# Gated mix of linear attention and a gated MLP: two buffers for x chunks, low parts in place, h blocks and last weights at other places of the order

## The chip, the cores and the metric

The kernel runs on one core of a Trainium2 chip, in one launch. The metric is device time in microseconds (us). The engines are named as in the profile: PE (TensorE matmul), DVE (VectorE), ACT (ScalarE), POOL (GpSimd) and SP (SyncE, which only issues DMAs here).

## The reference

The input `x` is 2048 tokens by 576. A linear attention with 32 heads of 18 and a gated MLP with 4608 hidden columns both read it, and a sigmoid gate mixes them.

```python
g = sigmoid((x * gate_w).sum(-1, keepdims=True))
q, k, v = heads(x @ wqkv)                      # 32 heads of 18
phi = lambda t: where(t > 0, t + 1, exp(t)) + 1e-6
kv = einsum("bhsd,bhse->bhde", phi(k), v);  z = phi(k).sum(s)
o = einsum("bhqd,bhde->bhqe", phi(q), kv) / (einsum("bhqd,bhd->bhq", phi(q), z) + 1e-6)
a = o.reshape(B, S, D) @ wo
b = (gelu(x @ w_gate) * (x @ w_up)) @ w_down
return g * a + (1 - g) * b
```

## The kernel before

All matrices are float32. The operands of PE are `float32r`, each split into a high part and a low part (value minus high part), and a product is summed from three of the four combinations. The three large products of the MLP use a seven-product scheme for 2x2 blocks (Strassen's, `PRODUCTS`, in the order of `SEQUENCE`): the sums of x blocks that it needs (S1 to S4), of weight blocks (T1 to T4) and of h blocks (S1 to S4 again) are formed on POOL and DVE.

The order of work on each engine is the order in which the program names it: nothing is rearranged, and each engine takes its instructions in that order. An instruction waits until its inputs are there and its output buffer is free, and all behind it on its engine wait too. DMAs issued by SP are in this order as well; a few are issued by ACT.

**The mixing stage** (lines 368 to 919). Queries of the four token blocks (512 tokens each, `query(b, g)` for five groups of heads), their denominators (`den`), the reciprocals of these, the scaled queries and the mixed output (`mixed(b, t)`, 128 tokens) are interleaved by hand, block 2 first, then 3, 0 and 1. `halves_of` splits a query for `den`. `reciprocals(b)` works on halves of a block: it stores a small tile to memory (L638) and reloads it spread over the rows of each head (L642, tile `rb`). `scaled` multiplies (L654) and splits (L65, L66) for `mixed` (PE, L673), whose result ACT scales by the gate and stores (`ga_d`, L678, L680).

Beside these, two things are prepared for the MLP:

* *Ahead chunks* 0 to 5: the sums of x blocks of the second half of the tokens, in pieces of 256 columns. `ahead_load(k)` loads a raw chunk (tile `xu`, two buffers, L388). `ahead_make(k)` forms the four sums in it on POOL (L378 to L381), copies high parts to `xuh` (L397, one buffer) and writes low parts to `xul` (L399, one buffer; for the chunks 4 and 5 into rows of `xuh`, L401). `ahead_store(k)` stores low (L408) and high parts (L409) to `xop_d`. `next_ahead(k)` is: store k-1, load k+1, make k.
* *Token chunks* 0 to 2 of the first half (tile `xc`, 128 x 4 x 512, one buffer, L608). `token_sums(kt, 0)` forms the sums on DVE; `token_sums(kt, 1)` copies high parts on ACT (L612) and low parts on POOL (L615) into `xo`, the operand of the first products.

`W[0]` and `W[1]`, the split and summed weights of gate and up, are loaded by ACT's queue for the first columns (L769, L912) into the place of the query weights.

**Gate and up** (lines 976 to 1012). `CHAINS` lists chains of seven products (L810), of GATE or UP, for token halves p = 0 and 1 and 18 pairs of column groups n; the last two chains are (1, 0, GATE) and (1, 0, UP), for which the weights of n = 0 come back from memory: `w_load(0)` behind the first product of chain LAST - 3, `w_load(1)` behind the last of LAST - 2, both on SP. Results of UP chains go to memory as h blocks (`h_d`, L841). `H_AT` names the places in the last two chains where the first four h blocks of the down product are split (`h_make`: ACT L978, DVE L979), each followed by a load of a later one (L973).

**Down** (lines 1013 to 1076). 84 units: six groups s of hidden columns, token halves p, seven products k; a unit is 36 matmuls (L1049) in two halves. Three units ahead, `h_make(u + 3)` splits an h block between the halves of a unit. The down weights of a group come in one load into `draw` (`d_fetch`, L955), are split and summed by `d_make(s, k)` (ACT copy L960, POOL low parts L962; for k = 0 also six POOL operations L965 that form sums in `draw` which later makes read; for k = 2 two). Products are accumulated on DVE (L1057), and ACT copies the result of the first product of a seven to a second bank (L1053).

Of the kernel before, what the change touches and what calls it, by code (L numbers as in the profile page):

```python
# [38 lines left out]
def tile_gated_mix(ctx, tc, xt, xs, xn, wk, wv, wq, wo, wgu, wdn, cst, out):  # L39
    nc = tc.nc  # L40
# [12 lines left out]
    def f32(ap):  # L53
        return ap.bitcast(F32)
# [318 lines left out]
    xup = mixing.pool("xup")  # L373
# [11 lines left out]
    def ahead_load(k):  # L385
        kt, c = k // 2, slice(k % 2 * 256, k % 2 * 256 + 256)
        raw = xup.tile([128, 4, 256], F32, name="xu", bufs=2)
        nc.sync.dma_start(raw, xs[1, kt, :, :, c])  # L388
        ahead[k] = [raw]

    def ahead_make(k):
        kt, (raw,) = k // 2, ahead[k]
        sum_blocks(raw, nc.gpsimd)
        hi = xup.tile([128, 4, 256], F32R, name="xuh")
        lo = xup.tile([128, 4, 256], F32R, name="xul") if kt < 2 else None
        for i in range(4):
            nc.gpsimd.tensor_copy(hi[:, i], raw[:, i])  # L397
            if kt < 2:
                nc.gpsimd.tensor_tensor(lo[:, i], raw[:, i], f32(hi[:, i]), OP.subtract)  # L399
            else:  # L400
                nc.gpsimd.tensor_tensor(hi[32:64, i], raw[32:64, i], f32(hi[32:64, i]), OP.subtract)  # L401
        ahead[k] = [hi, lo]

    def ahead_store(k):
        kt, c = k // 2, slice(k % 2 * 256, k % 2 * 256 + 256)
        hi, lo = ahead.pop(k)
        if kt < 2:
            nc.sync.dma_start(xop_d[:, S2:S1 + 1, 3 + kt, c], f32(lo))  # L408
        nc.sync.dma_start(xop_d[:, S2:S1 + 1, kt, c], f32(hi))  # L409

    def next_ahead(k):
        ahead_store(k - 1)
        if k < 5:
            ahead_load(k + 1)
        if k < 6:
            ahead_make(k)

# [159 lines left out]
    for k in range(2):  # L577
        ahead_load(k)
# [7 lines left out]
    for g in range(NG):  # L586
        if g + 1 < NG:
            query(3, g + 1)
        head_out(g)
        if g + 2 < NG:  # L590
            wo_load(g + 2)
        elif g + 2 == NG:
            for b, i, a in ((2, 0, A11), (2, 1, A12), (3, 1, A22)):
                nc.sync.dma_start(xop_d[:, a], f32(x_slot(b, i)))
        den(2, g)
        if g + 2 < NG:
            halves_of(2, g + 2)
    turn.close()
    weights.close()
    ahead_make(0)  # L600
# [26 lines left out]
    xcp = chunks.pool("xcp")  # L627
# [54 lines left out]
    chunk = [Chunk(xcp, 0, 0)]  # L682

    def token_load(kt):
        chunk[0] = Chunk(xcp, 0, kt)

    def token_sums(kt, part):
        if part == 0:
            chunk[0].sums()
        else:  # L690
            chunk[0].summed(nc.gpsimd)
# [3 lines left out]
    halves_of(3, 1)  # L695
    query(0, 0)
    query(0, 1)
    next_ahead(1)
# [4 lines left out]
    query(0, 2)  # L703
    den(3, 2)
# [4 lines left out]
    next_ahead(2)  # L709
    den(3, 4)  # L710
    scaled(2, 1)
    mixed(2, 0)
    reciprocals(3)
# [4 lines left out]
    next_ahead(3)  # L718
# [4 lines left out]
    query(1, 0)  # L723
    mixed(2, 2)
    ahead_store(3)
    ahead_load(5)
    token_load(1)
    ahead_make(4)
# [6 lines left out]
    mixed(2, 3)  # L735
    scaled(3, 1)
# [9 lines left out]
    ahead_store(4)  # L746
# [3 lines left out]
    token_load(2)  # L750
    ahead_make(5)
# [3 lines left out]
    query(1, 4)  # L755
    proj.close()
# [20 lines left out]
    ahead_store(5)  # L777
# [49 lines left out]
    def w_load(m):  # L827
        nc.sync.dma_start(f32(W[m]), wp_d[m])
# [154 lines left out]
    H_AT = [(LAST - 1, 1), (LAST - 1, 5), (LAST, 2), (LAST, 5)]  # L983
# [4 lines left out]
    for c, chain in enumerate(CHAINS):  # L988
        for i, step in enumerate(first_steps if c == 0 else gu_steps(*chain)):
# [10 lines left out]
            if i == 0 and c == LAST - 3:  # L1000
                w_load(0)
            if i == 6 and c == LAST - 2:
                w_load(1)
# [57 lines left out]
    for u, (s, p, k) in enumerate(UNITS):  # L1061
# [10 lines left out]
        if s < DG - 1:  # L1072
            if p == 0 and k == 3:
                d_fetch(s + 1)
            if p == 0 and k == 5:
                d_make(s + 1, 0)
# [65 lines left out]
```

## Time and profile before

| | |
|---|---|
| median of 3 runs | 1551.15 us (1545.82 to 1554.31) |
| the profiled execution | 1548.94 us, span 1547.2 us |
| busy time: PE, DVE, ACT, POOL | 1504.2 (97%), 1006.3 (65%), 539.0 (35%), 736.7 (48%) us |
| DMA | 248.19 MB, mean 160 GB/s |
| granted clock of PE, mean | 0.99 |

The page gives for each group of instructions its line, engine, output and inputs; the list of waits gives who stood for whom, with the total, the count and the longest in us. In a timeline a line is: start, duration (us), engine, line, operation, tiles and shapes, how many instructions are merged, and in brackets the idle time of that engine before it and what ended it. A row of windows is: the stretch, its length, busy time of PE, weight loads, DVE, ACT and POOL with their counts, the granted clock, the share of time in which the DMA engines were busy, and GB/s.

### The profile page before, as it was taken

The numbers are of one execution on the slowest core, as the hardware profiler recorded it, in microseconds if no ns is written. First come the engines' busy times: TensorE is split into PE (matmuls) and PEld (weight loads), VectorE is DVE, ScalarE is ACT, GpSimd is POOL, SyncE is SP. The second block draws the span as 40 slices with busy tenths as digits, with TensorE's granted clock in tenths as the row PEclk, the third lists the DMA queues.
The fourth block names the chain that finished last, engine by engine and source line by source line (L and its number), as shares of the span: only waits on it lengthen the run. The fifth ranks groups of instructions, "written<-read, shape, count | busy, mean of one in ns | idle before, by whom it ended". The sixth has DMA issues, their size and how long they took to land.

```text
span 1547.2 us, 21598 instructions
## 1 busy us (share of the span) xinstructions
PE 1504.2 (97%) x8354; PEld 1327.9 (86%) x8354; DVE 1006.3 (65%) x1314; ACT 539.0 (35%) x703; POOL 736.7 (48%) x560
## 2 busy tenths in 40 slices
PE   8999996799999999999999999999998999999999
PEld 8998875788788888888888888888788999999999
DVE  7886755456655666655566665556766776777775
ACT  6554543332233222223322223322244343534431
POOL 3653467164554454455456446444346282552700
PEclk9999997899999999999999999999999999999999
DMA  7554355574222333222233322233777656565664
GB/s 238 164 160 157 124 175 189 184 277 191 104 106 101 129 137 136 103 103 102 103 136 136 119 102 106 108 111 116 277 275 266 207 172 209 164 209 167 212 204 139
DMA packets 99310, 248.19 MB, mean 160 GB/s; under 512 B 8960, under 2 KB 38296, under 8 KB 96264
## 3 DMA queue, kind: packets, MB, share of 16 engines
q1 hardware_dynamic: 96328, 237.26, 44.6%
q10 hardware_dynamic: 2880, 9.57, 1.7%
q8 instruction: 65, 1.06, 0.3%
q14 instruction: 37, 0.30, 0.1%
HBM read 157.24 MB, written 89.55 MB: 160 GB/s over the span
## 4 chain that ended last, share of the span: by engine, by line
PE 83%; DMA 5%; DVE 3%; POOL 3%; issue 3%; ACT 1%; SPq 0%; DVEq 0%; POOLq 0%; ACTq 0%
PE bank L810 50%; PE bank L1049 24%; PE pair L244 2%; PE kpair L244 2%; DMA xc<-xs 1%; PE bank L432 1%; PE kpair L199 1%; PE pair L199 1%; POOL xul L399 1%; DMA stage<-wdn 1%; DMA rb<-rden_d 1%; POOL xuh L397 1%; PE pair L673 1%; DMA rden_d<-rb 1%; DMA wu<-wp_d 1%
## 5 line engine op out<-in xcount | busy, mean ns | idle before, releaser
L810 PE MATMUL bank<-xo,wg 128*128 128x512 f32 x1764 | 413.9, 395 | 3.2 <-DVE f L845 1.5
L810 PE MATMUL bank<-xo,wu 128*128 128x512 f32 x1764 | 412.8, 394 | 3.0 <-DMA wu<-wp_d 3.0
L810 PEld LDWEIGHTS bank<-xo,wg 128*128 128x128 f32 x1764 | 332.1, 189 | 81.1 <-DVE f L845 1.9
L810 PEld LDWEIGHTS bank<-xo,wu 128*128 128x128 f32 x1764 | 332.5, 189 | 80.3 <-DMA wu<-wp_d 3.5
L1057 DVE SCALAR_TENSOR_TENSOR acc<-bank,gate,acc 128x288 f32<-128x288 f32 x288 | 140.4, 511 | 76.0 <-PE bank L1049 67.6
L818 POOL TENSOR_TENSOR stage<-stage 128x384 f32<-128x384 f32 x136 | 159.6, 1193 | 46.7 <-DMA stage<-wgu 44.1
L824 POOL TENSOR_TENSOR wg<-stage,wg 128x768 fp32r<-128x768 f32 (+1 forms) x34 | 72.2, 2123 | 192.4 <-ACT wg L823 191.1
L854 ACT ACTIVATE p<-bank 128x512 f32<-128x512 f32 x72 | 43.2, 600 | 344.6 <-PE bank L810 344.6
L824 POOL TENSOR_TENSOR wu<-stage,wu 128x768 fp32r<-128x768 f32 (+1 forms) x34 | 79.7, 2344 | 146.2 <-ACT wu L823 144.9
L1049 PE MATMUL bank<-xo 128*128 128x288 f32 x1044 | 142.6, 296 | 4.8 <-DVE acc L1057 4.1
L1049 PEld LDWEIGHTS bank<-xo 128*128 128x128 f32 x1044 | 140.3, 189 | 5.3 <-DVE acc L1057 4.4
L962 POOL TENSOR_TENSOR wd<-stage,wd 128x432 fp32r<-128x432 f32 x40 | 58.4, 1483 | 130.8 <-ACT wd L960 130.7
L859 DVE TENSOR_TENSOR u<-bank,p 128x512 f32<-128x512 f32 x72 | 49.5, 687 | 99.5 <-PE bank L810 94.0
L1049 PE MATMUL bank<-wd,xo 128*128 128x288 f32 x792 | 106.8, 296 | 0.0
L1049 PEld LDWEIGHTS bank<-wd,xo 128*128 128x128 f32 x792 | 105.6, 188 | 0.0
L962 POOL TENSOR_TENSOR xo<-stage,xo 128x432 fp32r<-128x432 f32 x44 | 56.7, 1315 | 82.1 <-ACT xo L960 82.1
L845 DVE TENSOR_TENSOR e<-bank,u 128x512 f32<-128x512 f32 x54 | 37.3, 691 | 80.0 <-PE bank L810 79.7
L845 DVE TENSOR_TENSOR f<-bank,u 128x512 f32<-128x512 f32 x54 | 37.2, 691 | 76.1 <-PE bank L810 76.0
L835 ACT ACTIVATE f<-f 128x512 f32<-128x512 f32 x54 | 34.1, 632 | 140.9 <-DVE f L845 140.9
L673 PE MATMUL pair<-kw,p 126*128 126x288 f32 (+1 forms) x480 | 72.0, 310 | 8.2 <-ACT p L65 8.1
L673 PEld LDWEIGHTS pair<-kw,p 126*128 126x128 f32 (+1 forms) x480 | 70.3, 202 | 10.5 <-ACT p L65 8.5
L873 DVE TENSOR_TENSOR u<-bank,u 128x512 f32<-128x512 f32 x72 | 49.8, 691 | 38.8 <-PE bank L810 37.0
(189 smaller groups left out, 2315.9 us busy)
## 6 DMA issues: line engine op xcount, KB each, us to landing
h_d<-sx SPq DMA_DIRECT2D x108, 256.0 KB
stage<-wgu SPq DMA_DIRECT2D x34, 768.0 KB
xo<-h_d SPq DMA_DIRECT2D x29, 768.0 KB
e<-h_d SPq DMA_DIRECT2D x28, 768.0 KB
hraw<-h_d SPq DMA_DIRECT2D x27, 768.0 KB
h_d<-e SPq DMA_DIRECT2D x72, 256.0 KB
h_d<-f SPq DMA_DIRECT2D x72, 256.0 KB
stage<-wdn SPq DMA_DIRECT2D x6, 1728.0 KB
```

What stands on the lines that cost most here:

```text
L244: nc.tensor.matmul(y[:, n, :KH], a, p[:, n * KH:(n + 1) * KH], start=(k == 0), stop=(k == len(ops) - 1))
L673: nc.tensor.matmul(y[:, i, :288], p[:R, a, g], KW[g][:R, wl, i * 288:(i + 1) * 288], start=(n == 0), stop=(n == 14))
L810: nc.tensor.matmul(ps, w_, x_, start=start and i == 0, stop=i == 6, skip_group_check=not start)
L818: nc.gpsimd.tensor_tensor(o, a, b, OP.subtract)
L824: nc.gpsimd.tensor_tensor(w[:, i, 3:5], src[:, :, 0:2], f32(w[:, i, 0:2]), OP.subtract)
L845: nc.vector.tensor_tensor(es[i], a, b, OP.add)
L854: nc.scalar.activation(p1, ps["a"], AF.Copy)
L859: nc.vector.tensor_tensor(u2, b, p1, OP.add)
L873: nc.vector.tensor_tensor(u3, c, u2, OP.add)
L962: nc.gpsimd.tensor_tensor(w[:, 1, c], src[:, c], f32(w[:, 0, c]), OP.subtract)
L1049: nc.tensor.matmul(y, h[:, hl, g, t * 128:(t + 1) * 128], w[:, wl, g * 288:(g + 1) * 288], start=k in (1, 5) and n == 0, stop=n == len(ops ...
L1057: nc.vector.scalar_tensor_tensor(o, y, gate[:, 1, st:st + 1], o, op0=OP.mult, op1=OP.add)
```

## The change

* Mixing: `xcp` has two buffers, and `token_load(1)` and `token_load(2)` are issued earlier. `xul` is gone: low parts of the chunks 0 to 3 are written over the raw chunk and stored from there. The ahead pool moves to the place of the `raws` pool, next to the query weights, so its first two loads are issued once `raws` is closed. The stores of A12 and A22 to `xop_d` move from the loop before to behind `halves_of(3, 1)` and `query(0, 1)`. The places of makes, loads and stores in the order are others, and all go by `next_ahead`.
* End of gate and up: `H_AT` has later places, and `w_load(1)` is issued by ACT behind the first product of chain LAST - 1.
* Down: `d_fetch(s + 1)` is one unit later, and `d_make(s + 1, 0)` two units later, directly ahead of `d_make(s + 1, 1)`.
* `dynamic_dma_scratch_size` is 512 instead of 1024.

```diff
@@ -370,7 +370,6 @@
     mixing.banks(3)
     denp = mixing.psum("denp", 1)
     rp = mixing.pool("rp", bufs=2)
-    xup = mixing.pool("xup")
     made = Scope()
     r_of = {}
     def sum_blocks(raw, eng):
@@ -384,37 +383,33 @@
 
     def ahead_load(k):
         kt, c = k // 2, slice(k % 2 * 256, k % 2 * 256 + 256)
-        raw = xup.tile([128, 4, 256], F32, name="xu", bufs=2)
+        raw = xup.tile([128, 4, 256], F32, name="xu")
         nc.sync.dma_start(raw, xs[1, kt, :, :, c])
         ahead[k] = [raw]
 
     def ahead_make(k):
         kt, (raw,) = k // 2, ahead[k]
         sum_blocks(raw, nc.gpsimd)
-        hi = xup.tile([128, 4, 256], F32R, name="xuh")
-        lo = xup.tile([128, 4, 256], F32R, name="xul") if kt < 2 else None
+        hi = xup.tile([128, 4, 256], F32R, name="xuh", bufs=1)
         for i in range(4):
             nc.gpsimd.tensor_copy(hi[:, i], raw[:, i])
-            if kt < 2:
-                nc.gpsimd.tensor_tensor(lo[:, i], raw[:, i], f32(hi[:, i]), OP.subtract)
-            else:
-                nc.gpsimd.tensor_tensor(hi[32:64, i], raw[32:64, i], f32(hi[32:64, i]), OP.subtract)
-        ahead[k] = [hi, lo]
+            o = raw[:, i].bitcast(F32R) if kt < 2 else hi[32:64, i]
+            p = slice(0, 128) if kt < 2 else slice(32, 64)
+            nc.gpsimd.tensor_tensor(o, raw[p, i], f32(hi[p, i]), OP.subtract)
+        ahead[k] = [hi, raw]
 
     def ahead_store(k):
         kt, c = k // 2, slice(k % 2 * 256, k % 2 * 256 + 256)
         hi, lo = ahead.pop(k)
         if kt < 2:
-            nc.sync.dma_start(xop_d[:, S2:S1 + 1, 3 + kt, c], f32(lo))
+            nc.sync.dma_start(xop_d[:, S2:S1 + 1, 3 + kt, c], lo)
         nc.sync.dma_start(xop_d[:, S2:S1 + 1, kt, c], f32(hi))
 
     def next_ahead(k):
         ahead_store(k - 1)
         if k < 5:
             ahead_load(k + 1)
-        if k < 6:
-            ahead_make(k)
-
+        ahead_make(k)
 
     def wv_make(kt):
         raw = wv_raw.pop(kt)
@@ -574,8 +569,6 @@
 
     wo_load(0)
     wo_load(1)
-    for k in range(2):
-        ahead_load(k)
     query(2, 3)
     states_out()
     key_sums()
@@ -590,14 +583,16 @@
         if g + 2 < NG:
             wo_load(g + 2)
         elif g + 2 == NG:
-            for b, i, a in ((2, 0, A11), (2, 1, A12), (3, 1, A22)):
-                nc.sync.dma_start(xop_d[:, a], f32(x_slot(b, i)))
+            nc.sync.dma_start(xop_d[:, A11], f32(x_slot(2, 0)))
         den(2, g)
         if g + 2 < NG:
             halves_of(2, g + 2)
     turn.close()
     weights.close()
-    ahead_make(0)
+    aheads = Scope()
+    xup = aheads.pool("xup", bufs=2, side="right")
+    for k in range(2):
+        ahead_load(k)
 
     class Chunk:
 
@@ -624,7 +619,7 @@
     r3p = mixing.pool("r3p")
     qp = mixing.pool("qp", bufs=2)
     chunks = Scope()
-    xcp = chunks.pool("xcp")
+    xcp = chunks.pool("xcp", bufs=2)
 
     HB = BS // 2
 
@@ -679,53 +674,53 @@
                              scale=gate[:, 0, st:st + 1])
         nc.scalar.dma_start(ga_d[st], o)
 
-    chunk = [Chunk(xcp, 0, 0)]
+    chunk = {0: Chunk(xcp, 0, 0)}
 
     def token_load(kt):
-        chunk[0] = Chunk(xcp, 0, kt)
+        chunk[kt] = Chunk(xcp, 0, kt)
 
     def token_sums(kt, part):
         if part == 0:
-            chunk[0].sums()
+            chunk[kt].sums()
         else:
-            chunk[0].summed(nc.gpsimd)
+            chunk.pop(kt).summed(nc.gpsimd)
 
     halves_of(3, 0)
     reciprocals(2)
     halves_of(3, 1)
+    nc.sync.dma_start(xop_d[:, A12], f32(x_slot(2, 1)))
     query(0, 0)
+    ahead_make(0)
     query(0, 1)
-    next_ahead(1)
+    nc.sync.dma_start(xop_d[:, A22], f32(x_slot(3, 1)))
     den(3, 0)
     halves_of(3, 2)
     den(3, 1)
     halves_of(3, 3)
     query(0, 2)
+    next_ahead(1)
+    token_load(1)
     den(3, 2)
     halves_of(3, 4)
     den(3, 3)
     scaled(2, 0)
     query(0, 3)
-    next_ahead(2)
     den(3, 4)
     scaled(2, 1)
     mixed(2, 0)
+    next_ahead(2)
     reciprocals(3)
     query(0, 4)
     scaled(2, 2)
     token_sums(0, 0)
     mixed(2, 1)
-    next_ahead(3)
     halves_of(0, 0)
     halves_of(0, 1)
     scaled(2, 3)
     token_sums(0, 1)
     query(1, 0)
+    next_ahead(3)
     mixed(2, 2)
-    ahead_store(3)
-    ahead_load(5)
-    token_load(1)
-    ahead_make(4)
     den(0, 0)
     halves_of(0, 2)
     query(1, 1)
@@ -733,6 +728,8 @@
     den(0, 1)
     halves_of(0, 3)
     mixed(2, 3)
+    next_ahead(4)
+    token_load(2)
     scaled(3, 1)
     token_sums(1, 0)
     query(1, 2)
@@ -743,16 +740,16 @@
     scaled(3, 2)
     token_sums(1, 1)
     query(1, 3)
-    ahead_store(4)
+    next_ahead(5)
     den(0, 4)
     reciprocals(0)
     mixed(3, 1)
-    token_load(2)
-    ahead_make(5)
     scaled(3, 3)
     halves_of(1, 0)
     halves_of(1, 1)
     query(1, 4)
+    ahead_store(5)
+    aheads.close()
     proj.close()
 
 
@@ -774,7 +771,6 @@
     halves_of(1, 4)
     token_sums(2, 0)
     mixed(0, 0)
-    ahead_store(5)
     den(1, 4)
     scaled(0, 2)
     token_sums(2, 1)
@@ -824,8 +820,8 @@
             nc.gpsimd.tensor_tensor(w[:, i, 3:5], src[:, :, 0:2], f32(w[:, i, 0:2]), OP.subtract)
             nc.gpsimd.tensor_tensor(w[64:96, i, 2], src[64:96, :, 2], f32(w[64:96, i, 2]), OP.subtract)
 
-    def w_load(m):
-        nc.sync.dma_start(f32(W[m]), wp_d[m])
+    def w_load(m, queue):
+        queue.dma_start(f32(W[m]), wp_d[m])
 
     def gu_steps(p, n, m, first=False):
 
@@ -980,7 +976,7 @@
 
     XO2_AT = {(0, 4): (0, 1), (1, 1): (2,), (1, 4): (3,), (2, 1): (4,), (2, 4): (5,), (3, 1): (6,)}
     LAST = len(CHAINS) - 1
-    H_AT = [(LAST - 1, 1), (LAST - 1, 5), (LAST, 2), (LAST, 5)]
+    H_AT = [(LAST - 1, 3), (LAST - 1, 6), (LAST, 3), (LAST, 6)]
     at = {}
     for n in range(1, NF2):
         for m in range(2):
@@ -998,9 +994,9 @@
                 a = PRODUCTS[SEQUENCE[k]][0]
                 nc.sync.dma_start(f32(X[1][:, a]), xop_d[:, a])
             if i == 0 and c == LAST - 3:
-                w_load(0)
-            if i == 6 and c == LAST - 2:
-                w_load(1)
+                w_load(0, nc.sync)
+            if i == 0 and c == LAST - 1:
+                w_load(1, nc.scalar)
             if (c, i) == (LAST - 3, 1):
                 d_fetch(0)
             if (c, i) == (LAST - 2, 0):
@@ -1070,9 +1066,9 @@
         if u < 3:
             d_make(0, u + 4)
         if s < DG - 1:
-            if p == 0 and k == 3:
+            if p == 0 and k == 4:
                 d_fetch(s + 1)
-            if p == 0 and k == 5:
+            if p == 1 and k == 0:
                 d_make(s + 1, 0)
             if p == 1 and k < 6:
                 d_make(s + 1, k + 1)
@@ -1127,7 +1123,7 @@
         for r in range(GR[g]):
             cst[r, 126 + g * 64 + r // DH * NG + g] = 1.0
 
-    nc = bacc.Bacc("TRN2", target_bir_lowering=False, num_devices=1, dynamic_dma_scratch_size=1024)
+    nc = bacc.Bacc("TRN2", target_bir_lowering=False, num_devices=1, dynamic_dma_scratch_size=512)
     arrays, args = {}, []
     for name, a in (("xt", xt), ("xs", xs), ("xn", xn), ("wk", wk), ("wv", wv), ("wq", wq), ("wo", woh), ("wgu", wgu), ("wdn", wdn),
                     ("cst", cst)):
```

## The prediction

> **What bounds the kernel now.** I read the page, then the list of waits for PE, then the timelines of PE, DVE, POOL, ACT and SP around each wait.
>
> ```profile
> span 1547.2 us, 21598 instructions
> PE den L572 <- DVE hl L563: 16.2, 1, 16.2
> PE pair L673 <- ACT p L65: 8.1, 2, 6.1
> PE bank L1049 <- DVE acc L1057: 4.1, 1, 4.1
> PE bank L810 <- DMA wu<-wp_d: 3.0, 1, 3.0
> ```
>
> PE is the bound nearly everywhere, so only its few waits can be won. The two longest lie in the mixing stage, the other two around the change from gate/up to down. The PE timeline also shows what a wait costs afterwards:
>
> ```profile
> 221.34 4.14 PE L673 MATMUL pair<-kw,p 126*128 126x288 f32 x30
> 245.21 0.80 PE L572 MATMUL den<-hl,zmk 72*128 72x512 f32 x1 [16.22 <-DVE hl L563]
> 245.80 5.82 PE L673 MATMUL pair<-kw,p 126*128 126x288 f32 x30
> 264.83 4.36 PE L673 MATMUL pair<-kw,p 126*128 126x288 f32 x30
> 279.71 6.02 PE L673 MATMUL pair<-kw,p 126*128 126x288 f32 x30 [6.06 <-ACT p L65]
> 285.57 1.77 PE L810 MATMUL bank<-xo,wg 128*128 128x512 f32 x7
> 306.40 10.09 PE L673 MATMUL pair<-kw,p 126*128 126x288 f32 x60 [1.99 <-ACT p L65]
> ```
>
> The same 30 matmuls take 4.14 at full clock and 5.82 and 6.02 behind the waits: 1.7 and 1.9 more. Between 221.34 and the first product at 285.57, 16.2 + 6.1 + 1.7 + 1.9 = 25.9 us are lost. Why the engines behind stand:
>
> ```profile
> 235.23 0.36 SPq L608 DMA_DIRECT2D xc<-xs  x1
> 240.15 1.08 DVE L378 TENSOR_TENSOR xc<-xc 128x512 f32<-128x512 f32 x1 [14.35 <-DMA xc<-xs]
> 275.29 0.69 DVE L378 TENSOR_TENSOR xc<-xc 128x512 f32<-128x512 f32 x1 [6.37 <-DMA xc<-xs]
> ```
>
> One buffer holds a chunk, so chunk 1 is requested only at 235.23, when POOL is through with chunk 0. DVE reaches its sums 14.35 us early and stands in order, with the halves that PE needs behind them. Chunk 2 repeats it with 6.37.
>
> **The change, part 1: the mixing stage.** With a second chunk buffer `token_load(1)` is issued right behind chunk load 2, some 30 us earlier, and `token_load(2)` needs only POOL's end with chunk 0. Both waits on xc go. What is late next is the ahead chain, which SP and POOL walk together.
>
> ```profile
> 185.00:190.00 5.00, 5.00 (x23) 4.05 (x22) 2.82 (x5) 2.49 (x4) 1.26 (x2) 1.00 0.94 297
> 195.68 0.40 POOL L397 CAST xuh<-xu 128x256 fp32r<-128x256 f32 x1 [9.35 <-DMA xop_d<-xuh]
> 202.29 0.36 SPq L408 DMA_DIRECT2D xop_d<-xul  x1
> 204.16 1.76 SPq L638 DMA_DIRECT2D rden_d<-rb  x2
> 207.34 0.74 POOL L397 CAST xuh<-xu 128x256 fp32r<-128x256 f32 x1 [0.79 <-DMA xop_d<-xuh]
> 210.08 1.70 SPq L642 DMA_DIRECT2D rb<-rden_d  x2
> 217.90 0.81 DVE L654 SCALAR_TENSOR_TENSOR r<-r,rb 126x640 f32<-126x640 f32 x1
> ```
>
> The stores of A12 and A22 (each 128x5x512 float32, 1.31 MB) now stand ahead of the first ahead store, where chunk load 2 (0.52 MB) stood before. At the 297 GB/s of that stretch, 2.1 MB more are 7.1 us: xuh comes free at 202.8, not 195.68, and make 1 ends 7.1 after 202.29, at 209.4. There the second delay enters: the low parts now lie in the raw chunk, so load 3 must wait until low store 1 has *landed*. A pair of stores lands 5.05 us behind its issue (202.29 to 207.34), so I put the first of them at 3.2, and load 3 at 212.6. Queued behind it on SP stand the reciprocals of block 3: stored at 213.7, reloaded when that store has landed. That took 5.9 (204.16 to 210.08) with 1.5 MB ahead, and should take some 3.2 with two thirds of it, so the reload is issued at 216.9. Before, DVE used the reload without waiting 7.8 after its issue; I take 6.5 (from 4.5 to 7.8), 223.4 instead of 217.90. DVE stands, and halves 3 of block 0 follow 3.1 behind, at 226.5. PE wants them just ahead of 221.34: a wait of 5.7 (3 to 9), and 1.7 of slow clock.
>
> The rest of the chain runs on POOL:
>
> ```profile
> 230.28 4.92 POOL L615 TENSOR_TENSOR xo<-xc,xo 128x512 fp32r<-128x512 f32 x4
> 235.16 0.72 POOL L378 TENSOR_TENSOR xu<-xu 128x256 f32<-128x256 f32 x1
> 244.56 0.36 SPq L409 DMA_DIRECT2D xop_d<-xuh  x1
> 263.74 0.33 ACTq L769 DMA_DIRECT2D wg<-wp_d  x1
> ```
>
> A make takes 9.4 (235.16 to 244.56) and about one more for the xuh store; the low parts of a chunk take 4.92. From 209.4, make 2, chunk 0, make 3 and make 4 end at 245.2, and chunk 1 and make 5 at 260.4. The reciprocals of block 0 now stand on SP behind store 4: stored at 246, reload issued at 248.5, there at 255, scaled and split by 257.4. In the old run PE was ready for the last den of that block at 229.0 (245.21 - 16.22), and 264.83 lies 17.9 us of plain work behind it (19.6 less 1.7 of clock); with its lag of 7.4 PE wants the split at 254.3: a wait of 3.1, and 1.8 of clock.
>
> Then a wait that the diff doesn't show. By the shapes qwp holds 33280 bytes of a partition, W 35840 in the same place: 2560 more, which lay in `raws` (long free) and now lie in the ahead pool, in xuh if its tiles lie in order of first use. So the load of W[0], which ACT issued at 263.74, waits for store 5 to land, near 263, and ACT stands with it from 258, with halves 4 of block 1 behind. PE is through with the product at 263.3; ACT, released at 263, has three copies and DVE one operation of about 0.8 (L654's row) before those halves are there, at 266.4: 3.1 more. DVE's four sums (0.69) and the next split behind them cost another 0.9. Waits and clock together are 5.7 + 1.7 + 3.1 + 1.8 + 3.1 + 0.9 = 16.3 of the old 25.9: **9.6 us won**, the first product at 276.0. If none of these waits comes, all 25.9 are won; with the upper ends (7.8 a reload, and makes longer by a quarter through their stores), about 3. The 1.99 wait at 304.4 and its clock I leave as they are; they could go (3.7 more). Loads 0 and 1 go out later, which costs nothing: POOL, in order behind the low parts of wo, comes to make 0 no sooner than before (0.52 MB at 297 GB/s, 1.8 us, if it did). The smaller scratch costs nothing: no queue of POOL's stands in the page's list.
>
> [...]
>
> **Part 2: last weights, h blocks.**
>
> ```profile
> 1110.25 0.60 ACT L854 ACTIVATE p<-bank 128x512 f32<-128x512 f32 x1 [8.54 <-PE bank L810]
> 1116.62 8.16 DMA wu<-wp_d
> 1117.00:1126.00 9.00, 4.48 (x18) 3.01 (x18) 4.81 (x5) 4.63 (x6) 4.61 (x4) 1.00 0.98 371
> 1119.89 1.91 PE L810 MATMUL bank<-xo,wg 128*128 128x512 f32 x7 [1.49 <-DVE f L845]
> 1124.82 11.72 PE L810 MATMUL bank<-xo,wu 128*128 128x512 f32 x49 [3.03 <-DMA wu<-wp_d]
> ```
>
> On SP the load of W[1] stood behind the h stores until 1116.62. On ACT it follows the copy that ends at 1110.85; W[1] is free by then. 8.16 later it is there, at 1119.1, or at 1122.6 if the five stores (1.31 MB, 3.5 us at 371 GB/s) that now overlap it cost their full share. The h block that ran on DVE ahead of L845 moves behind it, so the wait of 1.49 goes and PE is ready for W[1] at 1120.0. The last chain starts between 1120.0 and 1122.6 instead of 1124.82: 2.2 to 4.8, taken as **3.0 won**. Later h blocks are loaded 1 to 3 us later and each is still ahead of its unit of products.
>
> [...]
>
> **Part 3: down weights.**
>
> ```profile
> L1057 DVE SCALAR_TENSOR_TENSOR acc<-bank,gate,acc 128x288 f32<-128x288 f32 x288 | 140.4, 511 | 76.0 <-PE bank L1049 67.6
> 1173.28 0.93 ACT L960 ACTIVATE wd<-stage 128x864 fp32r<-128x864 f32 x1 [10.43 <-DMA stage<-wdn]
> 1178.53 2.53 PE L1049 MATMUL bank<-xo 128*128 128x288 f32 x9 [4.13 <-DVE acc L1057]
> 1238.80 2.20 POOL L962 TENSOR_TENSOR wd<-stage,wd 128x432 fp32r<-128x432 f32 x2 [30.17 <-ACT wd L960]
> 1248.41 0.92 ACT L960 ACTIVATE wd<-stage 128x864 fp32r<-128x864 f32 x1
> 1249.22 1.48 ACT L978 ACTIVATE xo<-hraw 128x1536 fp32r<-128x1536 f32 x1
> 1250.91 2.28 DVE L979 TENSOR_TENSOR xo<-hraw,xo 128x1536 fp32r<-128x1536 f32 x1
> 1257.44 4.94 PE L1049 MATMUL bank<-xo,wu 128*128 128x288 f32 x36
> L965 POOL TENSOR_TENSOR stage<-stage x48: 1100/1121/2706, 1104.0 to 1459.0; 128x432 f32<-128x432 f32 x48
> ```
>
> In the first group ACT stood 10.43 us at `d_make(1, 0)` for its weights; h block and accumulation queued behind it, and PE lost 4.13, and 1.3 of clock (9 matmuls in 2.53 where 36 take 4.94). With the make two units later the weights are there: **5.4 won**, once.
>
> But `d_make(s+1, 0)` now stands directly ahead of `d_make(s+1, 1)`, whose ACT copy reads sums (DX) that POOL makes in the former. In the second group: ACT copy at 1248.41 (0.92), two POOL low parts (2.20), four of the six sums (4 x 1.12), the ACT copy that waited (0.92), the h block on ACT (1.48), its low part on DVE (2.28), the accumulation (0.51): 1261.2. PE wants that accumulation halfway through the unit of 1257.44, at 1259.8. So PE waits 1.4, in all five groups: **7.0 lost**. Ends: 0.9 (4.5) if DVE's low part takes no longer than the sums on POOL leave it, some 1.8; 3.0 (15) if one sum takes the maximum of 2.7; more with clock.
>
> **Sum.** 9.6 + 3.0 + 5.4 - 7.0 = 11.0 us. The profiled execution took 1548.94 (span 1547.2), 2.2 under the median of 1551.15: 1537.9 against its own time, 1540.1 against the median, so 1540.
>
> **Rivals.** *All of part 1 is won*: the reloads come in time and W[0] finds its place free. For it: 7.8 is only an upper bound, and the order of tiles is a guess. Against it: two new places behind stores on SP. 26 + 3 + 5.4 - 7 = 27, or 19 if one of the waits stays: 1524 to 1532, chance 0.19. *The waits only move*: makes a quarter longer, reloads at 7.8, W[1] no earlier than 1122.6. Part 1 gives 3, part 2 gives 2, part 3 nothing: 1545 to 1551, chance 0.25. *Slower, through the pairs of makes*: ACT stands behind POOL as it stood behind the DMA at 1173, and each of the five groups pays like that one, 5.4. That is 27 against 9.6 + 3.0 + 5.4: 9 slower, 1560. It decides when DX ends over about 4 us later than worked out, which two or three sums at 2.7 would do; for it speaks that this is how the 4.13 arose, against it that DVE, standing too, leaves POOL alone. Chance 0.15. The forecast, 1532 to 1545, has 0.41.
>
> **How the numbers follow.** A measurement of this kernel tells about 0.5%, 7.8 us, from no change. Faster: the forecast up to 1543.4 (0.38) and the first rival, 0.57. Same: the second and the forecast's edge, 0.28. Slower: 0.15. The range 1526 to 1556 leaves out the best of the first rival (0.06) and most of the third (0.13).
>
> **What would show it.** Right: no wait of DVE L378 on xc; instead waits of DVE L654 on rb near 223 and 255, ACT behind W[0]'s load near 260, the first product near 276; the last chain near 1122; five waits of PE on acc L1057, about 67 us apart, of 1 to 2 us. Wrong: a first product near 260 (the chain has slack) or behind 283 (it has none), or five waits on acc over 4 us.

## The result

| | before | after |
|---|---|---|
| median of runs on one chip | 1543.93 us (1538.81 to 1554.31, 11 runs) | 1558.28 us (1555.34 to 1561.28, 11 runs) |
| the profiled execution | 1548.94 us, span 1547.2 us | 1559.55 us, span 1557.8 us |
| busy PE, mean clock | 1504.2 us, 0.99 | 1511.2 us, 0.986 |

The change makes the kernel **slower by 0.86%**: the ratio of times is 1.0086, 95% interval 1.0064 to 1.0108. The prediction said 1540 us, and its range ended at 1556. Lines of `after` are 4 or 5 smaller than those of `before` (L673 is L668, L1049 is L1045, L1057 is L1053).

### The profile page after: what moved, and what is told of

The parts are those of the page before. It is cut to its first block, busy times and chain, and to the rows that moved or that the text cites. A ratio compares the mean times of both kernels' runs of the same rounds, so it can differ in the third digit from the quotient of the medians.

```text
span 1557.8 us, 21591 instructions
## 1 busy us (share of the span) xinstructions
PE 1511.2 (97%) x8354; PEld 1333.0 (86%) x8354; DVE 1005.9 (65%) x1314; ACT 539.3 (35%) x703; POOL 735.6 (47%) x560
## 4 chain that ended last, share of the span: by engine, by line
PE 75%; issue 2%; DVE 2%; POOL 1%; ACT 1%; DMA 1%; SPq 0%; ACTq 0%; DVEq 0%
PE bank L806 51%; PE bank L1045 22%; PE pair L668 2%; POOL stage L961 1%; POOL wd L958 0%; DMA acc<-ga_d 0%; ACT xo L974 0%; DVE f L834 0%; DVE acc L1053 0%; DMA ga_d<-ga 0%; DMA xop_d<-xuh 0%; ACT wd L956 0%; DVE u L844 0%; ACT ga L673 0%; POOL xo L958 0%
## 5 line engine op out<-in xcount | busy, mean ns | idle before, releaser
L1053 DVE SCALAR_TENSOR_TENSOR acc<-bank,gate,acc 128x288 f32<-128x288 f32 x288 | 137.0, 509 | 58.5 <-PE bank L1045 51.3
L1045 PE MATMUL bank<-xo 128*128 128x288 f32 x1044 | 143.6, 297 | 5.1 <-DVE acc L1053 3.8
L1045 PEld LDWEIGHTS bank<-xo 128*128 128x128 f32 x1044 | 141.0, 190 | 6.1 <-DVE acc L1053 4.3
L958 POOL TENSOR_TENSOR wd<-stage,wd 128x432 fp32r<-128x432 f32 x40 | 61.8, 1570 | 155.2 <-ACT wd L956 155.2
L1045 PE MATMUL bank<-wd,xo 128*128 128x288 f32 x792 | 107.7, 297 | 1.2 <-DVE acc L1053 1.2
L1045 PEld LDWEIGHTS bank<-wd,xo 128*128 128x128 f32 x792 | 106.4, 190 | 1.5 <-DVE acc L1053 1.5
L958 POOL TENSOR_TENSOR xo<-stage,xo 128x432 fp32r<-128x432 f32 x44 | 64.2, 1486 | 79.3 <-ACT xo L956 79.2
L668 PE MATMUL pair<-kw,p 126*128 126x288 f32 (+1 forms) x480 | 71.7, 311 | 9.8 <-ACT p L65 9.7
L668 PEld LDWEIGHTS pair<-kw,p 126*128 126x128 f32 (+1 forms) x480 | 70.9, 204 | 11.6 <-ACT p L65 10.2
```

Of the source, the lines that this page charges most:

```text
L668: nc.tensor.matmul(y[:, i, :288], p[:R, a, g], KW[g][:R, wl, i * 288:(i + 1) * 288], start=(n == 0), stop=(n == 14))
L958: nc.gpsimd.tensor_tensor(w[:, 1, c], src[:, c], f32(w[:, 0, c]), OP.subtract)
L1045: nc.tensor.matmul(y, h[:, hl, g, t * 128:(t + 1) * 128], w[:, wl, g * 288:(g + 1) * 288], start=k in (1, 5) and n == 0, stop=n == len(ops ...
L1053: nc.vector.scalar_tensor_tensor(o, y, gate[:, 1, st:st + 1], o, op0=OP.mult, op1=OP.add)
```

## The profile after

The list of waits for PE in the changed kernel (who waited for whom; us in total, how often, the longest):

```profile
PE bank L1045 <- DVE acc L1053: 15.0, 5, 8.7
PE pair L668 <- ACT p L65: 9.7, 1, 9.7
PE den L567 <- ACT hl L557: 8.4, 2, 6.2
```

The waits of the mixing stage, 16.2 for DVE and 8.1 for `p` before, are now 8.4 and 9.7, and that for `wu` is gone. The wait of the down stage for `acc` went from one of 4.1 to five with 15.0 together. Where they lie, from PE's timeline of the changed kernel:

```profile
228.86 0.80 PE L567 MATMUL den<-hl,zmk 126*128 126x512 f32 x1 [6.23 <-ACT hl L557]
268.02 6.21 PE L668 MATMUL pair<-kw,p 126*128 126x288 f32 x30 [9.73 <-ACT p L65]
276.40 1.73 PE L567 MATMUL den<-hl,zmk 72*128 72x512 f32 x2 [2.16 <-ACT hl L557]
288.02 1.78 PE L806 MATMUL bank<-xo,wg 128*128 128x512 f32 x7
315.62 4.64 PE L806 MATMUL bank<-xo,wg 128*128 128x512 f32 x19 [0.83 <-ACT ga L673]
...
1130.96 3.90 PE L1045 MATMUL bank<-xo 128*128 128x288 f32 x27
1185.88 3.61 PE L1045 MATMUL bank<-xo 128*128 128x288 f32 x18 [2.57 <-DVE acc L1053]
1263.12 4.69 PE L1045 MATMUL bank<-xo,wu 128*128 128x288 f32 x18 [8.66 <-DVE acc L1053]
1334.12 2.64 PE L1045 MATMUL bank<-xo,wg 128*128 128x288 f32 x18 [1.25 <-DVE acc L1053]
...
1470.72 2.66 PE L1045 MATMUL bank<-wd,xo 128*128 128x288 f32 x18 [1.23 <-DVE acc L1053]
```

The same two places in PE's timeline of before:

```profile
317.31 5.10 PE L810 MATMUL bank<-xo,wg 128*128 128x512 f32 x21 [0.83 <-ACT ga L678]
...
1136.38 3.74 PE L1049 MATMUL bank<-xo 128*128 128x288 f32 x27
```

Three pieces follow from these rows. Up to the last chain of the mixing stage the changed kernel is 1.7 us ahead (317.31 to 315.62), though this execution began the stage 1.8 us late (the `wos` low part of L512, at 172.37 for 170.59; PE has the 1.8 already at 34 us of the span, ahead of anything the change touches). At the first down product it is 5.4 us ahead (1136.38 to 1130.96). From there to the end of the span the changed kernel needs 1557.8 - 1131.0 = 426.8 us where before needed 410.8: **16.0 us lost in the down stage**. Of these the waits for `acc` are 15.0 less 4.1; most of the rest is the clock, seen in the windows of 50 us behind the long wait (behind the window's length stands PE's busy time with its matmuls; 0.91 is the granted clock), first of the changed kernel:

```profile
1260.00:1310.00 50.00, 46.88 (x333) 46.89 (x334) 38.78 (x52) 18.51 (x17) 8.02 (x7) 0.91 0.55 175
```

and the same of before:

```profile
1260.00:1310.00 50.00, 50.00 (x379) 50.00 (x379) 37.62 (x49) 19.34 (x19) 15.36 (x13) 1.00 0.60 206
```

46 matmuls fewer are 6.1 us at 50 / 379 each, and only 3.1 of them are idle time. The other 3.0 are the slower clock.

## Experiments

Each time is the median beside that of the kernel before on the same chip; the ratio to it has its 95% interval.

### Which part loses: four kernels on one chip (before: 1545.12 us)

**makes_back**: the changed kernel with its third part undone.

```diff
-            if p == 0 and k == 4:
+            if p == 0 and k == 3:
                 d_fetch(s + 1)
-            if p == 1 and k == 0:
+            if p == 0 and k == 5:
                 d_make(s + 1, 0)
```

> The changed kernel with its third part undone: the fetch of the next down weights and the first make stand where they stood before. Theory of the pairs (two makes one behind the other cost the down stage about 16 us: five waits of PE for acc, 15.0 us in all, and about 3 us of slower clock behind them, against the 4.1 us wait of before): 1541 to 1544 us, the waits for acc at 1242, 1334, 1402 and 1470 us gone, one of about 4 us at 1174 us back. Rival, the 8.7 us wait is an accident of the profiled execution and a pair costs 1.25 us: about 1553 us. Rival, the loss lies ahead of the down stage (mixing): no less than 1555 us.

Measured 1545.81 us, 1.0005 (0.9990 to 1.0020), 1.8 above the 1541 to 1544 expected. The list of waits:

```profile
PE bank L1045 <- DVE acc L1053: 4.7, 2, 4.5
```

The one of 4.5 is back, at 1175.73, and those from 1242 on are gone. The theory of the pairs holds, both rivals fall: a pair that cost 1.25 would have left 1553.

**makes_only**: the same edit the other way round, in the kernel before.

> The kernel of before with the third part alone. Theory of the pairs: 16 us slower than before, 1558 to 1562 us, with the five waits for acc. Rival, a pair costs 1.25 us: 1544 to 1549 us. Rival, the loss needs the mixing or the later h blocks too: no slower than before.

Measured 1556.79 us, 1.0077 (1.0048 to 1.0106): 11.7 us slower, somewhat less than the 16 expected and just under the 1558 to 1562, with the same five waits and, in DVE's timeline, the same long low part of h as in the changed kernel (below). The list of waits and then rows of the timelines:

```profile
PE bank L1049 <- DVE acc L1057: 13.6, 5, 8.7
```

```profile
281.25 1.78 PE L810 MATMUL bank<-xo,wg 128*128 128x512 f32 x7
310.75 5.11 PE L810 MATMUL bank<-xo,wg 128*128 128x512 f32 x21 [0.83 <-ACT ga L678]
...
1250.09 9.89 DVE L979 TENSOR_TENSOR xo<-hraw,xo 128x1536 fp32r<-128x1536 f32 x1 [7.28 <-ACT xo L978]
```

This kernel has the mixing stage of before, unchanged, and the first two rows are a second look at it: its last chain starts at 310.75, 6.6 us earlier than in the profile of before that the prediction was built on, and its waits for `p` sum to 3.3 instead of 8.1.

**mixing_only**: the first part alone (H_AT, the load of W[1], `d_fetch` and `d_make` as before).

> The changed kernel with its second and third parts undone, so the first part (two chunk buffers, low parts in place, stores moved) alone. From the changed kernel's trace, whose first gate and up product on the second half came 1.7 us earlier than before although its stage began 1.8 us later: 1540 to 1543 us. If the prediction's sum for the mixing stage held (9.6 us): 1534 us. If its waits only move: 1543 to 1546 us.

Measured 1547.64 us, 1.0018 (1.0001 to 1.0034). The first part wins nothing; it is 2.5 us above before's median, where 9.6 below was forecast. 1540 to 1543, read off the changed kernel's trace, missed too, since that trace was held against a profile of before with a late mixing stage, and even the case that the waits only move ended at 1546. Between this kernel and makes_back lies only the second part: 1.8 us won in the medians, with intervals that overlap.

**makes_apart**: the changed kernel, with the first make one unit ahead of the second instead of directly ahead.

```diff
-            if p == 1 and k == 0:
+            if p == 0 and k == 6:
                 d_make(s + 1, 0)
```

> The changed kernel with the first make of the next weights one group of products earlier (p 0, k 6), a group of 9.5 us ahead of the next make, so that GpSimd's 8.7 us of it are over when ScalarE comes to the next copy. Theory of the pairs: the waits for acc from 1242 us on are gone, the one at about 1183 us stays at 2 to 4 us because there both makes still wait for the fetch that lands at 1173 us; 1540 to 1543 us. Rival, the fetch one group later is what costs: waits for acc stay and the time is over 1550 us.

Measured 1545.02 us, 1.0008 (0.9987 to 1.0028), in place of 1540 to 1543; its runs go from 1541.1, the profiled one, to 1551.5. Its list of waits:

```profile
PE bank L1045 <- DVE acc L1053: 0.9, 1, 0.9
```

Only this wait for `acc` is left: the pair is what costs, not the later fetch. With all pairs gone this kernel is no faster than before, so the first part's gain is missing as well.

### What a pair does

The timelines of ACT, POOL and DVE in the second group of the changed kernel, and one row of the third:

```profile
1250.41 0.93 ACT L956 ACTIVATE wd<-stage 128x864 fp32r<-128x864 f32 x1 [6.61 <-POOL stage L961]
...
1246.04 6.50 POOL L961 TENSOR_TENSOR stage<-stage 128x432 f32<-128x432 f32 x6
1252.50 2.20 POOL L958 TENSOR_TENSOR wd<-stage,wd 128x432 fp32r<-128x432 f32 x2
...
1258.88 2.14 POOL L958 TENSOR_TENSOR xo<-stage,xo 128x432 fp32r<-128x432 f32 x2
...
1252.74 9.89 DVE L975 TENSOR_TENSOR xo<-hraw,xo 128x1536 fp32r<-128x1536 f32 x1 [7.28 <-ACT xo L974]
1262.56 1.78 DVE L1053 SCALAR_TENSOR_TENSOR acc<-bank,gate,acc 128x288 f32<-128x288 f32 x4
...
1331.13 2.50 DVE L975 TENSOR_TENSOR wu<-e,wu 128x1536 fp32r<-128x1536 f32 x1 [7.25 <-ACT wu L974]
```

ACT stands 6.61 us for the sums on POOL, as foreseen. Then the low part of h on DVE starts 0.24 us behind an operation of POOL and lasts 9.89 us: it ends 1.6 us behind POOL's eight operations in a row (1252.50 to 1261.0). In the third group it starts as closely behind POOL and takes 2.50. In the profile of before no operation of DVE of this form lasts over 2.62, in that of the changed kernel none but this one over 2.50. To see whether POOL's burst is the cause:

**lows_on_vector**: the changed kernel with the low parts of the down weights on DVE.

```diff
         for c in (slice(0, 432), slice(432, 864)):
-            nc.gpsimd.tensor_tensor(w[:, 1, c], src[:, c], f32(w[:, 0, c]), OP.subtract)
+            nc.vector.tensor_tensor(w[:, 1, c], src[:, c], f32(w[:, 0, c]), OP.subtract)
```

> The changed kernel with the low parts of the down weights made on VectorE instead of GpSimd, all else as in it: the pairs of makes stay. VectorE gets about 1.2 us more per make, GpSimd keeps only the differences. If the 9.9 us of VectorE's low part of h at 1252 us (1.75 us elsewhere) are its wait while GpSimd runs eight operations in a row, it takes 1.8 to 3 us now, PE's 8.7 us wait for acc there falls to 1 to 2 us, and the time to 1548 to 1552 us. If GpSimd's burst has nothing to do with it, the 8.7 us wait stays and the time is 1556 to 1560 us. ScalarE still waits about 6.6 us in each pair for the differences in either case.

Measured 1557.52 us, 1.0077 (1.0063 to 1.0092; before 1545.92). The list of waits, and the row of DVE in the second group:

```profile
PE bank L1045 <- DVE acc L1053: 11.2, 15, 1.8
```

```profile
1260.06 1.75 DVE L975 TENSOR_TENSOR xo<-hraw,xo 128x1536 fp32r<-128x1536 f32 x1
```

The operation takes 1.75 again and PE's 8.66 has become 0.73, as the theory said. The time lies where the rival had it, at 1556 to 1560, so the trace speaks for the burst and the time does not. Five waits of 0.6 to 1.8 stay at the pairs, and ten new ones of 0.3 and 1.05 come behind them, which fits a DVE that is now late. The down stage is 5.9 us shorter (420.9), but in this execution, the slowest of its six, all of that was spent ahead of it: the mixing stage, whose code is the same, ends 4.7 later, and gate and up take 3.9 more, with ACT's `p` at the last chain 3.2 late instead of 1.3. The burst fits as the cause of the long operation; since the edit also shifted the timing, that it is the cause is not shown beyond that.

### Where the mixing gain went

The timelines of mixing_only, which has no late start:

```profile
218.20 1.72 SPq L637 DMA_DIRECT2D rb<-rden_d  x2
...
220.64 0.49 SPq L406 DMA_DIRECT2D xop_d<-xuh  x1
...
253.07 0.36 SPq L406 DMA_DIRECT2D xop_d<-xuh  x1
...
232.46 0.40 POOL L395 CAST xuh<-xu 128x256 fp32r<-128x256 f32 x1 [2.93 <-DMA xop_d<-xuh]
246.40 0.42 POOL L395 CAST xuh<-xu 128x256 fp32r<-128x256 f32 x1 [3.13 <-DMA xop_d<-xuh]
...
263.08 0.83 DVE L649 SCALAR_TENSOR_TENSOR r<-r,rb 126x640 f32<-126x640 f32 x1 [9.49 <-DMA rb<-rden_d]
...
264.73 6.54 PE L668 MATMUL pair<-kw,p 126*128 126x288 f32 x30 [8.99 <-ACT p L65]
...
271.02 0.33 ACTq L766 DMA_DIRECT2D wg<-wp_d  x1
...
285.50 1.77 PE L806 MATMUL bank<-xo,wg 128*128 128x512 f32 x7
```

The high store of step 2, issued at 220.64 behind the reload of block 3 (218.20), frees `xuh` only at 232.46, 11.8 us later. Make 3 ends at 240.1 where the prediction's sum has 235, make 4 at 253.07 where it has 245. So the reload of block 0, behind store 4, reaches DVE at 263.08 and not at 255, and W[0]'s load goes out at 271.02, not at 263. Three places can be relieved: the reloads that stand behind ahead steps on SP, W[0]'s place in SBUF, and the two stores ahead of store 0. The following kernels all start from makes_apart. The first four of them ran on another chip than it did (before there: 1545.69 us). Runs of one kernel spread here by up to 16 us, as those of makes_apart do by 10, so a profiled execution can lie 7 us off its median; why is not shown, and a difference of 7 us between medians is just clear of the intervals or touches them.

**reloads_first**: reciprocal groups ahead of the steps.

```diff
+    reciprocals(3)
     next_ahead(2)
-    reciprocals(3)
...
-    next_ahead(5)
     den(0, 4)
     reciprocals(0)
+    next_ahead(5)
```

> makes_apart with the two reciprocal groups ahead of the ahead steps that stand in front of them on SyncE (reciprocals 3 ahead of step 2, reciprocals 0 ahead of step 5). Both reloads start 7 to 12 us earlier, since their data were there at 199.8 and 245.6 us. Theory that the load of W[0] is the last wait (its place in SBUF is still held by the last high parts, whose store is issued at 267.6 us whatever the reloads do, and ScalarE stands behind it): PE's waits of 6.3 and 8.4 us go, one of 10 us or more comes ahead of a product that needs ScalarE, the first gate and up product stays at 283 to 286 us, and the time at 1543 to 1546 us. Rival, the reloads alone set the stage: first product near 271 us and about 1531 us.

Measured 1552.01 us, 1.0038 (1.0026 to 1.0049): 7 us *slower* than makes_apart in the medians, first product at 290.52. The rival fell, and the theory's 1543 to 1546 missed as well. From its timelines:

```profile
207.59 1.64 SPq L637 DMA_DIRECT2D rb<-rden_d  x2
...
209.89 0.52 SPq L406 DMA_DIRECT2D xop_d<-xuh  x1
...
222.34 0.40 POOL L395 CAST xuh<-xu 128x256 fp32r<-128x256 f32 x1 [8.86 <-DMA xop_d<-xuh]
...
254.36 1.15 ACT L557 ACTIVATE hl<-r 126x512 fp32r<-126x512 f32 x2 [12.25 <-DMA xu<-xs]
```

The reload now lies ahead of high store 1, which frees `xuh` 12.4 us after its issue (before the edit POOL waited 1.1 there), and make 2 ends 10.7 late (230.3 for 219.6), about as much as the reload came early (207.59 for 217.62). Make 5 still starts 3.7 late. The second reload, of block 0, did not come earlier at all (257.19 for 255.95). Then comes a wait that no estimate had: ACT's store of `ga`, ready at 242.1, goes out at 253.99, and the trace names the load of a raw chunk on SP (issued at 249.63) as what ended ACT's 12.25 us. So a store of ACT stood here for a load on SP's queue, one that is itself late; why it stands for that load is not shown.

**order_of_tiles**: the three tiles named in another order when the pool is first used, so that W[0] overlaps the raw chunk of the even steps.

```diff
+    xu_of = {}
...
+        if not xu_of:
+            for n in ("xuh", "xu1", "xu0"):
+                xu_of[n] = xup.tile([128, 4, 256], F32R if n == "xuh" else F32, name=n, bufs=1)
-        raw = xup.tile([128, 4, 256], F32, name="xu")
+        raw = xu_of[f"xu{k % 2}"]
...
-        hi = xup.tile([128, 4, 256], F32R, name="xuh", bufs=1)
+        hi = xu_of["xuh"]
```

> makes_apart with the three tiles of the ahead steps in another order in SBUF, so that W[0] lies over the raw chunk of step 4 (read for the last time at 252.7 us) and not over the high parts, whose last store is issued at 267.6 us. By the theory ScalarE no longer stands ahead of W[0]'s load (7.2 us idle before it went out), PE's wait of 2.7 us for hl goes, and the wait of 8.4 us for the reload stays: first product at 282 to 283 us, 2 to 3 us off the time, 1542 to 1543 us.

Measured 1537.96 us, 0.9952 (0.9935 to 0.9968): 7 us faster than makes_apart, more than twice what was expected; reloads_and_tiles against reloads_first, on one chip, gives the same 7. PE in makes_apart:

```profile
273.44 1.73 PE L567 MATMUL den<-hl,zmk 72*128 72x512 f32 x2 [2.68 <-ACT hl L557]
274.98 10.41 PE L668 MATMUL pair<-kw,p 126*128 126x288 f32 x60
285.22 1.77 PE L806 MATMUL bank<-xo,wg 128*128 128x512 f32 x7
```

and ACT's queue and PE in order_of_tiles:

```profile
263.98 0.33 ACTq L771 DMA_DIRECT2D wg<-wp_d  x1
...
271.39 8.12 PE L673 MATMUL pair<-kw,p 126*128 126x288 f32 x60
279.35 1.78 PE L811 MATMUL bank<-xo,wg 128*128 128x512 f32 x7
```

The load goes out at 263.98 instead of 270.56, the wait for hl is gone, and 60 matmuls take 8.12 instead of 10.41: a wait of 2.7 cost another 3.4 in clock (2.3 here, 1.1 in the two matmuls at 273.44).

**reloads_and_tiles**: both.

> Both of the above. By the theory of two waits behind one another both gains appear only together: waits of 6.3, 8.4 and 2.7 us gone, first product at 270 to 276 us, 10 to 14 us faster than makes_apart, 1531 to 1535 us. Rival, a third wait (the makes on GpSimd, or the low parts of the chunks) takes their place: 1538 us or more.

Measured 1545.00 us, 0.9985 (0.9966 to 1.0003). The rival holds: as in reloads_first, 7 us slower than without the earlier reloads. The profiled execution, 1537.6, is one of its fastest and no slower than that of order_of_tiles, 1538.8, so the traces don't show the 7.

**stores_early**: and the stores of A12 and A22 back in the loop.

```diff
-            nc.sync.dma_start(xop_d[:, A11], f32(x_slot(2, 0)))
+            for b, i, a in ((2, 0, A11), (2, 1, A12), (3, 1, A22)):
+                nc.sync.dma_start(xop_d[:, a], f32(x_slot(b, i)))
```

(and the two single stores left out).

> reloads_and_tiles with the stores of A12 and A22 back in the loop of head outputs, as before. They no longer lie ahead of the first low and high stores, which landed 15.9 us after their issue; the makes run about 12 us earlier. If the makes still bound the mixing in reloads_and_tiles: up to 5 us faster than it. If they do not: the same within 2 us.

Measured 1538.10 us, 0.9951 (0.9932 to 0.9970): 7 us faster than without, a little over the 5 expected; here too the profiled executions (1541.3, without 1537.6) don't show it. ACT still stands 13.8 us with `ga`, now by the trace for a load of `xc` on SP.

On a third chip (before 1545.92 us), without the earlier reloads:

**stores_only**: makes_apart with this edit alone.

> makes_apart with only the stores of A12 and A22 back in the loop. By the same theory the makes and with them the last high store are 6 to 12 us earlier, so W[0]'s load is too, and the reloads: 1533 to 1540 us, 5 to 12 us faster than makes_apart. Rival, the stores do not bound the makes: 1545 us as makes_apart.

Measured 1538.28 us, 0.9949 (0.9936 to 0.9962): 7 us again, inside what was expected. W[0]'s load goes out at 262.66 instead of 270.56. PE still loses 6.5 at 265.55 to ACT, which stands 9.2 us ahead of W[0]'s load; the trace names the last high store as what ended it.

**tiles_and_stores**: the order of the tiles and the early stores.

> makes_apart with the three tiles in the other order and the stores of A12 and A22 back in the loop of head outputs; the reciprocal groups stay where the change has them. Theory that the reloads stand behind load 3, which waits for low store 1, which waits for the makes, which wait for high store 0 behind the two stores: without these the makes run 6 to 12 us earlier, PE's waits of 6.3 and 7.4 us shrink to 3 us or less each, the first product comes at 268 to 274 us, and the time is 1528 to 1534 us. Rival, the makes are bound by GpSimd itself and not by the stores: no faster than order_of_tiles, 1537 to 1540 us.

Measured **1527.52 us, 0.9888** (0.9874 to 0.9903, 4 runs), faster than both kernels and just ahead of the expected 1528 to 1534. Its PE list keeps of the two mixing waits

```profile
PE den L572 <- DVE hl L563: 3.2, 3, 1.4
PE pair L674 <- ACT p L65: 2.5, 3, 1.2
```

and its timelines show why:

```profile
205.53 0.94 SPq L639 DMA_DIRECT2D rden_d<-rb  x2
...
254.06 0.33 ACTq L770 DMA_DIRECT2D wg<-wp_d  x1
...
268.81 1.78 PE L810 MATMUL bank<-xo,wg 128*128 128x512 f32 x7
298.28 5.11 PE L810 MATMUL bank<-xo,wg 128*128 128x512 f32 x21 [0.83 <-ACT ga L679]
```

Reciprocals 3 go out at 205.53 instead of 213.89 with no edit of their place, since load 3 ahead of them, which waits for low store 1, goes out at 204.89 instead of 213.19; `xuh` comes free for make 1 at 195.04 instead of 201.62. W[0] goes out at 254.06, and the first product starts at 268.81, earlier than the forecast 276.0. The two edits give 17.5 us against makes_apart on another chip, more than the 7 of each alone.

**all_three**: and the low parts of the down weights on DVE.

> tiles_and_stores with the low parts of the down weights on VectorE. Without pairs GpSimd's bursts are covered, so by the theory of the pairs nothing is left to win in the down stage beyond the 2 to 3 us that its first weights still cost: the same as tiles_and_stores within 3 us. If VectorE becomes late by the added 1.2 us per make: up to 5 us slower.

Measured 1531.59 us, 0.9912 (0.9899 to 0.9926): 4 us slower than tiles_and_stores, with intervals that overlap a little, so which of the two cases it is stays open. In the profiled executions 2.5 of the 4.6 lie in the mixing stage, whose code is the same (last chain at 300.78 for 298.28), and 2.0 in the down stage (412.2 for 410.1), where PE's wait for ACT's copy of a bank grew from 2.2 to 2.9.

## Why the prediction was wrong

By parts, forecast and measured, in us won: mixing 9.6 and -2.5; last weights and h blocks 3.0 and 1.8; down weights -1.6 (5.4 less 7.0) and -11.7. These three measured parts sum to -12.4, and the direct comparison says -14.3. The forecast failed twice, by 12.1 in the mixing stage and by 10.1 at the down weights.

*Down weights.* The step that failed is the sum for the second group, in one term: "its low part on DVE (2.28)". Up to it the chain came as worked out: ACT released by the fourth sum, copy, h block on ACT. But DVE's operation took 9.89 while POOL worked on, the accumulation ended 20.2 us behind the first ACT copy (1242.88 to 1263.08) instead of 12.8, and PE stood 8.66, not 1.4. The prediction took 2.28 for it and 1.8 at the lower end, and looked for a larger loss only in longer sums on POOL. Three of the other groups came out at 1.23 to 1.25, near 1.4; the first, where both makes stand behind the fetch that arrives at 1173, at 2.57. The term 5.4 for the old stall was too large as well: ACT's stand for the fetch shrank from 10.43 to 1.26, but makes_apart, with the later fetch and no pairs, still loses 2.0 and 0.9 at that place, and its down stage is only 1.1 shorter than that of before (409.7 for 410.8). The clock behind 8.66 and 2.57 was left out of the sum. The rival "Slower, through the pairs of makes" had the sign and, with 1560, nearly the time, but by another account: it let all five groups pay 5.4 by sums of 2.7, while POOL's sums were 1.08 each and one group paid most.

*Mixing.* The two waits on xc are gone, as forecast, and the first half of the chain came within 1.3 us: make 1 ended at 209.6 (209.4), load 3 at 213.7 (212.6), the reload of block 3 issued at 218.2 (216.9) and on DVE at 224.7 (223.4), PE's wait 6.4 (5.7). Some of that is luck: the 202.8 for `xuh` (201.9 measured) takes off 0.52 MB for chunk load 2, which before issued behind the store and not ahead of it (184.42, the store 183.88); without that the same sum gives 204.5.

The step that failed is "A make takes 9.4 (235.16 to 244.56) and about one more for the xuh store": makes 3 and 4 took 15.1 and 13.0. High store 2, which make 3 waits for, lay behind 1.29 MB of the reload that the paragraph before had just placed there and freed `xuh` after 11.8 us. Make 4 waited 3.13 for store 3, which took 5.8 with no reload ahead. The 5.05 us for a pair of stores came from a place without a reload ahead of it, and 9.4 was the shortest make of that profile. The profile of before had the other case, too:

```profile
225.15 0.90 POOL L397 CAST xuh<-xu 128x256 fp32r<-128x256 f32 x1 [7.57 <-DMA xop_d<-xuh]
```

There `xuh` came free 10.6 us after the issue of its store (214.58), which stood behind a reload (210.08). From the longer makes both later waits end 8 us late: the reload of block 0 reaches DVE at 263.1 (255), which costs PE 9.0 (3.1), and the load of W[0] goes out at 271.0 (263). The first product is at 285.5 (276.0). The text named 283 as the point from which the chain has no slack. That W[0] waits for store 5 through its place in SBUF, called a guess, is shown by order_of_tiles (263.98 for 270.56); and that the two stores delay `xuh`, by tiles_and_stores (195.04 for 201.62 in makes_apart).

*The base.* Part of the 25.9 us to be won was of one execution. Two profiles of the same mixing code (before, makes_only) have their last chain at 317.3 and 310.8, and before's runs go from 1538.8 to 1554.3. Against its later medians of 1543.9 to 1545.9 the profiled 1548.94 was slow by 3 to 5. The changed mixing stage spreads as much: in the five profiles that have it unaltered, that chain starts between 313.6 and 320.3, so no single profile prices it.

*Last weights.* Right: no wait for `wu` is left, the last chain waits 1.3 for ACT instead. The medians give 1.8 against 3.0, not clear of the noise; the traces say it better. From the last chain of the mixing stage to the first down product, before, makes_only and mixing_only need 819.1 to 821.6 us, and the changed kernel, makes_back and makes_apart 815.3 to 816.3. Some 0.7 of that is lost again at the next wait, for `u` (1.3 for 0.6).

*The clock.* The prediction gives the wait of 1.99 a loss in clock of its own (3.7 with the wait), and the traces agree: in the profile of before the granted clock is 1.00 from 300.0 to 304.0 and 0.65 in the 4 us behind that wait (306.4 to 310.4). Of the same 60 matmuls, those behind a wait of 1.25 in tiles_and_stores take

```profile
288.89 8.56 PE L674 MATMUL pair<-kw,p 126*128 126x288 f32 x60 [1.25 <-ACT p L65]
```

and those behind 1.62 in order_of_tiles

```profile
299.83 9.86 PE L673 MATMUL pair<-kw,p 126*128 126x288 f32 x60 [1.62 <-ACT p L65]
```

With 0.60 (8.54), 0.81 (8.57), 1.29 (8.55), 1.78 (9.93), 3.23 (10.82), 3.40 (10.49) and 3.69 (10.98) from other runs, all at this place of the program, the loss sets in here between 1.3 and 1.6 us of idle time.

## What to carry to other kernels

When a store or load is moved to another place of a queue, follow what then lies ahead of each later transfer and give it that many bytes: here a 5 us landing became 12 behind a reload, and the whole chain of makes paid. Two preparations that share an engine should not be queued directly behind one another, even where each is covered alone: one unit between them was worth 12 us. Which tile lies under a later weight load decides when it may start; the order in which a pool's tiles are first named moved that start from 270.56 to 263.98, and the time by 7 us.

## What the runs showed of the hardware

* An operation of DVE (1.75 us in lows_on_vector) lasted 9.89 us while POOL ran eight operations back to back at 1.07 us each, in the changed kernel and in makes_only, at the same place of both. In the other four groups of the changed kernel, started as closely behind POOL (0.24 us), it took 2.47 to 2.50, and POOL's operations took 1.85 each instead. That the burst of eight holds up the operation is what the two rows of 9.89 suggest, with lows_on_vector in favour; what decides between the two cases is open.
* A wait of 2.7 us, 30 matmuls behind one of 8.4, cost 3.4 us more in clock (makes_apart against order_of_tiles; granted from 264 to 286 us were 0.71 and 0.87). Behind a single wait the same 60 matmuls (8.38 us without a wait) took 8.57 at most up to 1.29 us of idle time, and 9.86 behind 1.62 us to 10.98 behind 3.69 us.
